# Routing counts by four token columns per product in a fused attention, expert and feed-forward kernel

## The chip, the cores and the metric

The kernel runs on one core of one Trainium2 chip. The metric is the device time of one execution in microseconds (us). An execution is also recorded by the hardware profiler: its span runs from the first to the last instruction. The engines are TensorE (PE in the rows; its weight loads are PEld), VectorE (DVE), ScalarE (ACT), GpSimd (POOL) and SyncE (SP, which issues most transfers).

## The reference

```python
def _moe_ref(x, w_gate, w1, w2):          # x: output of a causal attention with a window of 64
    N, D = x.shape                        # 2304 tokens, 512
    E = w_gate.shape[1]                   # 8 experts
    cap = N // E                          # 288
    flat = (x @ w_gate).flatten()
    order = np.argsort(-flat)
...
    for idx in order:                     # greedy over all (token, expert) pairs
        tok, e = (int(idx) // E, int(idx) % E)
        if assigned[tok] >= 0 or counts[e] >= cap:
            continue
        assigned[tok] = e
        counts[e] += 1
...
    for e in range(E):
        mask = assigned == e
        h = np.maximum(x[mask] @ w1[e], 0.0)
        out[mask] = h @ w2[e]

def _moe2_ref(x, w_in, w_out):            # 512 to 2048 to 512
    h = x @ w_in
    return np.maximum(0.01 * h, h) @ w_out
```

The attention has 4 batches of 8 heads of 576 tokens, 64 wide; each expert is 512 to 1024 to 512.

## The kernel before, in words

**Stages.** The attention takes the first 85 us or so of the span. Then come eight experts, e0 to e7, with 288 tokens each, and the dense feed-forward over blocks of those tokens, m0 to m4, in the order e0 e1 m0 e2 e3 m1 e4 e5 m2 e6 e7 m3 m4. An expert has eight steps, a dense block sixteen. In a step of an expert TensorE does 12 products of 288 columns for `h` and 12 for `ya`; in a step of a block, 12 products of 512 columns for `h` and 12 for `oa` (the weights are `w` or `res`). Each fp32 product is done as three such products, after DVE, ACT or POOL have split the weights into a high and a low part; e0 alone takes its weights unsplit, `w_raw`, in plain fp32.

**Routing.** The greedy assignment is done exactly in eight phases, 0 to 7; phase k fixes the tokens of one more expert, and its gather list must be there before that expert's tokens (`xg`) are fetched by POOL. Tokens lie as 128 partitions by `NT` = 18 columns. A phase below 7 looks for a threshold of each token's key in six rounds, r = 0 to 5. In a round with r of 1 or more:

- DVE compares every key with up to 31 digits: the grid `r_G` (128x558, from `r_E`, the rest of the key, and the last digit in PSUM), and then makes the next `r_E`;
- TensorE counts by expert: one product with `r_nrem` and then 18, one for each token column, whose stationary operand is a 128-column window of the grid and whose moving operand is that column's eight-wide one-hot of the expert, `r_oh`; all add up in one PSUM tile `rp` (128x8);
- DVE makes `r_sat` of it with a scan, and one product with `pow` gives the next digit, again a tile `rp`.

So the chain of a round is: `pow` product, grid and `r_E` on DVE, a burst of 19 products, a scan, the next `pow` product. There is one PSUM buffer for `rp`. A phase ends with a tail on DVE and small products (`r_tot`, `r_OB`, `r_ids`). Round 0 compares the top of the key with 127 values, in pieces along the columns (`cuts`).

**Who sets the order.** No engine looks ahead past a waiting instruction, and the kernel is issued in one hand-made order. `Clocks` keeps a time for each engine as instructions are issued, `cost()` being its price list; `RouteDriver.tick()`, called between the big products, reads these times and puts in the next piece of routing when the model says that its input is ready. `Router.phase` is a generator: `yield 'p'` means that a piece for TensorE comes next, `'v'` one for DVE that waits for TensorE, `'d'` one for DVE that waits for nothing. `tick()` also places pieces of `Convert` (splitting the dense weights) and evacuations. Nearly everything after the attention goes through the helper line L1267, so the rows are told apart by tile names.

Of the kernel before, what the change touches and what calls it, by code (L numbers as in the profile page):

```python
# [8 lines left out]
BF = mybir.dt.bfloat16  # L9
# [4 lines left out]
PSUM = bass.MemoryType.PSUM  # L14
# [3 lines left out]
NT = 18  # L18
# [293 lines left out]
class Router:  # L312
# [3 lines left out]
    def __init__(self, nc, pool, pp, L, cf, ci, cb, ones_b, pow2):  # L316
        self.nc, self.pool, self.pp = nc, pool, pp
        self.cf, self.ci, self.tri, self.iota, self.ones, self.pow2 = cf, ci, cb['tri'], cb['iota'], ones_b, pow2
        self.Lm, self.nps = L, 0
        self.base = pool.tile([128, 2, 8], F32, name="r_base")  # L320
        self.uw = pool.tile([128, 8], F32, name="r_uw")
        self.slotg = pool.tile([128, NT], F32, name="r_slotg")
        self.nrem = pool.tile([128, 8], BF, name="r_nrem")
        self.sel = [pool.tile([128, 128], BF, name=f"r_sel{k}") for k in range(2)]
        for k, x in enumerate(self.sel):
            nc.gpsimd.memset(x, 0.0)
            for p in range(2):
                nc.gpsimd.memset(x[32 * p:32 * p + 1, 1 - k:], 1.0)
        nc.gpsimd.memset(self.sel[0][64:65, 0:1], 1.0)
        self.comb = pool.tile([128, 3], F16, name="r_comb")  # L330
        self.combb = cb['comb']
        self.M = pool.tile([128, 6, NT], I32, name="r_M")
        self.k = pool.tile([128, 2, NT], I32, name="r_k")
        self.spread, self.cont = cb['spread'], cb['cont']
        self.sat = pool.tile([128, 8], BF, name="r_sat")
        self.G = [pool.tile([128, n * NT], BF, name=f"r_G{k}") for k, n in enumerate((128, 38))]
        self.OB = [pool.tile([128, 18 * (n - 1) + 128], F16, name=f"r_OB{n}") for n in (9, 18)]
        for x in self.G + self.OB:
            nc.gpsimd.memset(x, 0.0)
        self.ip = pool.tile([128, 128], F16, name="r_ip")  # L340
# [6 lines left out]
    def start2(self):  # L347
        v, cf = self.nc.vector, self.cf
        v.tensor_copy(self.uw, cf['ew'])
        v.tensor_scalar(out=self.nrem, in0=self.base[:, 0], scalar1=cf['na'], scalar2=cf['nb'], op0=ALU.mult, op1=ALU.add)  # L350
        v.tensor_copy(self.comb, self.combb)
    def ps(self, p, n, apart=False):

        self.nps += 1
        if apart:
            return self.p0.tile([128, 4, 96], F32, tag="xt", name=f"rq{self.nps}", bufs=1).rearrange("p a b -> p (a b)")[:p, :n]
        return self.pp.tile([128, 128], F32, tag="rp", name=f"rp{self.nps}")[:p, :n]
    def t(self, shape, dt, name, ph):
        bufs = {"E": 2, "ids": 8, "eidx": 8}.get(name, 1)
        return self.pool.tile(shape, dt, tag="r_" + name, name=f"r_{name}_{ph}", bufs=bufs)  # L360
# [53 lines left out]
    def phase(self, ph, out):  # L414
# [7 lines left out]
        def b3(ap, n, last):  # L422
            return ap.unsqueeze(2).to_broadcast([128, n, last])
        def bm(ap, n, last):
            return ap.unsqueeze(1).to_broadcast([128, n, last])
        if ph:
            m = t([128, NT], F32, "m", ph)
            v.tensor_reduce(out=m, in_=Lm, axis=AX.X, op=ALU.max)
            eqw = self.eqw0
            TT(out=eqw, in0=Lm, in1=b3(m, NT, 8), op=ALU.is_equal)  # L430
            yield 'd', 0
            TT(out=eqw, in0=eqw, in1=bm(cf['ew'], NT, 8), op=ALU.mult)
            mxw = t([128, NT], F32, "mxw", ph)
            v.tensor_reduce(out=mxw, in_=eqw, axis=AX.X, op=ALU.max)
            OH = t([128, NT, 8], BF, "oh", ph)
            TT(out=OH, in0=eqw, in1=b3(mxw, NT, 8), op=ALU.is_equal)
            yield 'd', 0
        else:
            m, OH, mxw = self.first
        E = dig = None  # L440
        if ph < 7:
            for r in range(6):
                J = 127 if r == 0 else NB[r - 1]
                jw = 128 if J > 32 else 32
                rows = slice(128 - jw, 128 - jw + J)
                GE, win = (self.ge0, self.win0) if ph + r == 0 else self.grid(r % 2, jw)
                pc, c0 = None, 0
                cuts = (0, 18) if ph + r == 0 else (0, 9, 15, 18) if ph == 0 else (0, 9, 18) if r == 0 else (0, 18)
                for lo, hi in zip(cuts, cuts[1:]):
                    w = hi - lo  # L450
                    if r:
                        STT(out=GE[:, lo:hi, :J], in0=b3(E[:, lo:hi], w, J), scalar=dig, in1=bm(cf[f'jt{r - 1}'], w, J), op0=ALU.subtract, op1=ALU.is_ge)
                    elif ph:
                        TT(out=GE[:, lo:hi, :J], in0=b3(m[:, lo:hi], w, J), in1=bm(ci['t1'].bitcast(F32), w, J), op=ALU.is_ge)
                    if hi < NT:
                        yield 'p' if ph == 0 else 'd', 0
                    if hi < NT and ph:
                        continue
                    if hi == NT:
                        if r:  # L460
                            En = t([128, NT], F32, "E", f"{ph}_{r}")
                            if r < 5:
                                STT(out=En, in0=E, scalar=dig, in1=self.M[:, r + 1], op0=ALU.subtract, op1=ALU.add)
                            else:
                                TS(out=En, in0=E, scalar1=dig, scalar2=None, op0=ALU.subtract)
                            E = En
                        elif ph:
                            E = t([128, NT], F32, "E", f"{ph}_0")
                            for _ in self.keys(m, 0, NT, False):
                                pass  # L470
                            self.rest(E)
                        else:
                            E = self.e0
                        yield 'p', 0
                    if pc is None:
                        pc = self.ps(128, 8, ph == 0)
                        nc.tensor.matmul(pc, self.sel[r > 0], self.nrem, start=True, stop=False)
                    for c in range(c0, hi):
                        nc.tensor.matmul(pc, win(c), OH[:, c, :], start=False, stop=(c == NT - 1))
                    c0 = hi  # L480
                yield 'v', 1
                v.tensor_tensor_scan(self.sat[rows], pc[rows], self.ones[rows, :8], 0.0, ALU.max, ALU.min)
                if ph + r == 0:
                    self.rest(E)
                yield 'p', 0
                pa = self.ps(128, 8)
                nc.tensor.matmul(pa, self.pow2[r], self.sat, start=True, stop=True)
                dig = pa[:, 7:8]
                yield 'v', 0
# [692 lines left out]
class Clocks:  # L1182
# [21 lines left out]
    def cost(self, e, name, out, ins):  # L1204
        n = [int(np.prod(x.shape[1:])) for x in [out] + ins]
        psum = any(x.space == PSUM for x in [out] + ins)
        if "dma" in name:
            return 1050 if "indirect" in name else 550 if e == "gpsimd" else 60
        if name == "transpose":
            return n[0] * 0.85  # L1210
        if e == "tensor":
            return max(n[0] * (1.68 if ins[0].dtype == F32 and ins[1].dtype == F32 and ins[1].shape != ins[0].shape else 0.447) + 1, 25)
        n = max(n)
        if e == "scalar":
            return n * 0.833 * (2.9 if out.dtype == F16 else 1) + (55 if psum else 140)
        if e == "gpsimd":
            return n * 2.2 + 98
        big = [x for x in ins if x.shape[-1] > 1]
        fast = not psum and (len(big) < 2 or all(x.dtype == BF for x in big + [out])) and "reduce" not in name
        return n / (1.92 if fast else 0.96) + 66  # L1220
# [4 lines left out]
    def charge(self, e, name, a, kw):  # L1225
# [15 lines left out]
        if e == "tensor":  # L1241
            small = int(np.prod(out.shape[1:])) <= 32
            if self.small and not small:
                end = self.at[e] = end + 90
            self.small = small
        by = e
        if "dma" in name:
# [103 lines left out]
def build(nc, tc, qT, kT, v, vT, wg, cfd, cid, cbd, w12, wio, out):  # L1351
    with ExitStack() as ctx:
# [36 lines left out]
                next(slow, None)  # L1389
        rp = ctx.enter_context(tc.tile_pool(name="rp", bufs=1))  # L1390
        rt = Router(nc, rp, None, L, cf, ci, cb, ones, make_pow2(nc, rp))
        ahead = {5: (0, 6), 11: (6, 12), 14: (12, 15), 17: (15, 18)}
        queue = []
        def done(c):
# [62 lines left out]
```

## Time and profile before

| | |
|---|---|
| time, median of 3 executions | 777.53 us (776.45 to 777.86) |
| time of the profiled execution | 772.07 us |
| its span | 770.4 us |
| mean granted TensorE clock | 0.985 |
| TensorE busy | 735.4 us, 95% of the span |
| TensorE weight loads busy | 622.3 us, 81% |
| VectorE busy | 437.9 us, 57% |
| ScalarE busy | 335.5 us, 44% |
| GpSimd busy | 172.9 us, 22% |

The profiled execution lies 5.46 us under the median of the three timed ones. Busy times are sums over all stages; TensorE's includes time in which products overlap in its pipeline, so pitches (start to start) are read rather than durations.

### The profile page before, as it was taken

How to read it: one execution, taken by the hardware profiler on the slowest of the kernel's cores; microseconds unless marked ns; L12 is line 12 of the kernel's file. 1: busy time of each engine (PE TensorE's matmuls, PEld its weight loads, DVE VectorE, ACT ScalarE, POOL GpSimd, SP SyncE). 2: the span in 40 equal slices, each digit the busy share in tenths (PEclk: the TensorE clock that was granted, in tenths of full speed). 3: DMA queues.
4: the chain of work that ended last, by engine and by line, in shares of the span. 5: the costliest groups of instructions: out<-in, count | busy, mean ns of one | idle time of the engine just before them, and what ended most of it. 6: DMA issues, size and time to landing. Idle time of an engine off the chain costs nothing.

```text
span 770.4 us, 15241 instructions
## 1 busy us (share of the span) xinstructions
PE 735.4 (95%) x5905; PEld 622.3 (81%) x5906; DVE 437.9 (57%) x1110; ACT 335.5 (44%) x736; POOL 172.9 (22%) x263
## 2 busy tenths in 40 slices
PE   6999669999999999999999999999999999999996
PEld 4777436798777789997788899888889998888895
DVE  3798888898899889885832423222233223222332
ACT  4898816566876344432122445222244532121321
POOL 6253130302000024300000598100038830000201
PEclk9999869999999999999999999999999999999999
DMA  9996167624585647362144364622436462324752
GB/s 347 408 412 271 56 213 257 230 75 168 193 268 208 240 159 221 115 220 83 55 164 163 93 211 142 219 91 101 163 110 223 137 219 83 110 76 170 246 180 94
DMA packets 40087, 138.56 MB, mean 180 GB/s; under 512 B 4942, under 2 KB 5966, under 8 KB 40016
## 3 DMA queue, kind: packets, MB, share of 16 engines
q1 hardware_dynamic: 35280, 123.21, 45.7%
q0 software_dynamic: 4304, 14.16, 5.5%
q8 instruction: 46, 0.75, 0.4%
q10 hardware_dynamic: 432, 0.23, 0.1%
q14 instruction: 25, 0.20, 0.1%
HBM read 117.66 MB, written 19.92 MB: 179 GB/s over the span
## 4 chain that ended last, share of the span: by engine, by line
PE 78%; DVE 14%; DMA 4%; issue 2%; ACT 1%; SPq 0%; POOLq 0%; POOL 0%; DVEq 0%; ACTq 0%
PE h L1267 35%; PE oa L1267 24%; PE ya L1267 10%; DVE r_G L1267 3%; PE rp L1267 3%; PE ao L165 2%; DVE w L1267 2%; DMA cv_in<-in_wio_dram 1%; DMA avt<-in_vt_dram 1%; PE apt L150 1%; DVE amx L137 1%; PE xtp L1267 1%; DMA ak<-in_k_dram 1%; PE as L130 1%; PE warm L1267 1%
## 5 line engine op out<-in xcount | busy, mean ns | idle before, releaser
L1267 DVE SCALAR_TENSOR_TENSOR h<-h,tg 128x512 f32<-128x512 f32 (+1 forms) x80 | 51.5, 644 | 149.1 <-ACT tg L1267 148.8
L1267 PE MATMUL h<-Y,w 128*128 128x512 f32 (+1 forms) x600 | 135.3, 371 | 0.0
L1267 PE MATMUL oa<-w,hh 128*128 128x512 f32 x540 | 133.0, 392 | 0.0
L1267 ACT COPY tg<-h 128x512 f32<-128x512 f32 (+1 forms) x80 | 43.6, 545 | 187.6 <-PE h L1267 175.1
L1267 PEld LDWEIGHTS h<-Y,w 128*128 128x128 f32 x600 | 104.2, 188 | 18.6
L1267 PEld LDWEIGHTS oa<-w,hh 128*128 128x128 f32 x540 | 99.7, 188 | 20.0
L1267 POOL TENSOR_TENSOR w<-raw,w 128x512 fp32r<-128x512 f32 x53 | 66.8, 1293 | 207.9 <-DMA raw<-in_w_dram 107.2
L1267 PE MATMUL ya<-hh,w 128*128 128x288 f32 x672 | 99.8, 296 | 0.6 <-DVE hh L1267 0.6
L1267 PE MATMUL h<-xT,w 128*128 128x288 f32 x672 | 100.0, 297 | 0.0
L1267 PEld LDWEIGHTS h<-xT,w 128*128 128x128 f32 x672 | 92.5, 188 | 0.6
L1267 PEld LDWEIGHTS ya<-hh,w 128*128 128x128 f32 x672 | 92.0, 188 | 0.8 <-DVE hh L1267 0.8
L1267 PE MATMUL h<-Y,res 128*128 128x512 f32 (+1 forms) x360 | 82.8, 374 | 0.0
L1267 PE MATMUL oa<-res,hh 128*128 128x512 f32 x324 | 82.2, 398 | 0.0
L1267 POOL DMA_INDIRECT out_dram<-ot,sidx x18 | 19.5, 1082 | 238.5 <-DVE ot L1267 135.6
L1267 DVE TENSOR_TENSOR hh<-h,hh 128x512 fp32r<-128x512 f32 (+1 forms) x80 | 51.0, 637 | 38.5 <-ACT hh L1267 38.3
L1267 PEld LDWEIGHTS h<-Y,res 128*128 128x128 f32 x360 | 62.3, 188 | 12.3
L1267 ACT CAST hh<-h 128x512 fp32r<-128x512 f32 (+1 forms) x80 | 43.6, 545 | 63.9 <-DVE h L1267 63.9
L1267 PEld LDWEIGHTS oa<-res,hh 128*128 128x128 f32 x324 | 59.6, 188 | 13.1 <-ACT hh L1267 0.4
L1267 ACT ACTIVATE hh<-h 128x288 fp32r<-128x288 f32 (+1 forms) x64 | 26.5, 413 | 92.1 <-PE h L1267 90.1
L1267 ACT CAST w<-raw 128x512 fp32r<-128x512 f32 x112 | 64.1, 619 | 0.0
L1267 DVE SCALAR_TENSOR_TENSOR hh<-h,hh 128x288 fp32r<-128x288 f32 x56 | 25.4, 454 | 63.4 <-ACT hh L1267 63.2
L145 ACT ACTIVATE ap<-as,anm 128x128 f32<-128x128 f32 x144 | 41.9, 402 | 17.4 <-DVE anm L138 11.8
(171 smaller groups left out, 935.4 us busy)
## 6 DMA issues: line engine op xcount, KB each, us to landing
w<-wsp SPq DMA_DIRECT2D x80, 512.0 KB, 3.9
raw<-in_w_dram SPq DMA_DIRECT2D x53, 512.0 KB, 4.1
cv_in<-in_wio_dram SPq DMA_DIRECT2D x32, 512.0 KB, 5.2
wsp<-w SPq DMA_DIRECT2D x20, 512.0 KB, 3.7
avo<-in_v_dram SPq DMA_DIRECT2D x6, 876.0 KB, 9.9
aq<-in_q_dram SPq DMA_DIRECT2D x12, 384.0 KB, 9.7
avt<-in_vt_dram SPq DMA_DIRECT2D x6, 768.0 KB, 9.9
xd<-ax SPq DMA_DIRECT2D x18, 256.0 KB, 7.7
```

Of the source, the lines that this page charges most:

```text
L130: nc.tensor.matmul(S[64 * t:64 * t + 64, a, u, :].rearrange("p (b c) -> p b c", b=2), q[h], k[h], start=False, stop=True, skip_group_check ...
L137: nc.vector.tensor_reduce(out=mx, in_=S[:, a:a + n], axis=AX.X, op=ALU.max)
L145: nc.scalar.activation(p[:, u, :], S[:, a, u, :], AF.Exp, bias=nm[a][:, u:u + 1], scale=0.125)
L150: nc.tensor.transpose(pt[:, u, :], p[:, u, :], ident)
L165: nc.tensor.matmul(o[64 * t:64 * t + 64, h // 4, h % 4, :], ptb[:, u, 64 * t:64 * t + 64], (ve, vo)[t][m][:, s, h, :], start=True, stop=Tr ...
L1267: return f(*a, **kw)
```

## The change

Three things in `Router`, and the price list of the model that orders everything:

- In phases 2 to 6, rounds 1 to 5 (25 rounds), the burst of 19 products becomes two bursts of five. The first, A, multiplies a window of the grid with the one-hots of four token columns at once (32 columns; the last product 16); of its 128x32 result only a shifted diagonal counts. ACT copies the result to `r_cq` as f16, and the second burst, B, is the `r_nrem` product and four products with shifted identities (`r_shift`), which add up the diagonal in the 128x8 tile. Other products run between A and B. `r_shift` is filled once, by GpSimd and DVE, during the attention.
- Three small DVE operations on the keys move from behind round 0's grid to between the operations ahead of it, in phases 1 to 6; round 0's grid is made in three pieces instead of two.
- `Clocks.cost` gets other prices for DVE scans and strided reads, for operations with a scalar in PSUM and for small f16 outputs on ACT; a big product behind a small one is charged 30 ns, not 90.

```diff
@@ Router.__init__ / start2
+        self.shift = pool.tile([128, 224], F16, name="r_shift")
+        nc.gpsimd.memset(self.shift, 0.0)
...
+        v.tensor_copy(self.shift[:, 96:], self.ident)
@@ Router.phase
             eqw = self.eqw0
+            ks = self.keys(m, 0, NT, False) if ph < 7 else iter(())
             TT(out=eqw, in0=Lm, in1=b3(m, NT, 8), op=ALU.is_equal)
+            next(ks, 0)
             yield 'd', 0
             TT(out=eqw, in0=eqw, in1=bm(cf['ew'], NT, 8), op=ALU.mult)
+            next(ks, 0)
...
-                cuts = (0, 18) if ph + r == 0 else (0, 9, 15, 18) if ph == 0 else (0, 9, 18) if r == 0 else (0, 18)
+                cuts = (0, 18) if ph + r == 0 else (0, 9, 15, 18) if ph == 0 else (0, 6, 12, 18) if r == 0 else (0, 18)
...
-                            for _ in self.keys(m, 0, NT, False):
-                                pass
                             self.rest(E)
...
+                    if ph > 1 and r:
+                        pb = self.ps(128, 32)
+                        for k in range(0, NT, 4):
+                            n = min(4, NT - k)
+                            nc.tensor.matmul(pb[:, :8 * n], self.G[r % 2][:, 96 + 32 * k:224 + 32 * k], OH[:, k:k + n, :], start=(k == 0), stop=(k >= NT - 6), skip_group_check=True)
+                        yield 'v', 1
+                        cq = t([128, 32], F16, "cq", f"{ph}_{r}")
+                        nc.scalar.copy(cq, pb)
+                        yield 'p', 0
+                        pc, c0 = self.ps(128, 8), hi
+                        nc.tensor.matmul(pc, self.sel[1], self.nrem, start=True, stop=False)
+                        for k in range(4):
+                            nc.tensor.matmul(pc, self.shift[:, 32 * k:32 * k + 128], cq[:, 8 * k:8 * k + 8], start=False, stop=(k == 3))
@@ Clocks.cost / charge
-            return n * 0.833 * (2.9 if out.dtype == F16 else 1) + (55 if psum else 140)
+            return n * 0.833 * (2.9 if out.dtype == F16 and n > 100 else 1) + (55 if psum else 140)
...
+        if "scan" in name or max((x.ap[-1][0] for x in ins if x.shape[-1] > 1), default=1) > 4:
+            return n * 2.1 + 66 if n > 100 else n + 66
+        if any(x.space == PSUM and x.shape[-1] == 1 for x in ins):
+            return n / 0.96 + 140
...
-                end = self.at[e] = end + 90
+                end = self.at[e] = end + 30
```

TensorE in block m1, a round of phase 6, before (`rp_5537` is the count of round 2; 17 more pairs like the last one follow, the number behind a row is how many follow one another):

```order
L1267 LDWEIGHTS pow_1_93
L1267 MATMUL rp_5524<-r_sat,pow_1_93 128x8
L1267 MATMUL oa_2_5485<-res_72,hh_5462 128x512
L1267 MATMUL oa_3_5486<-res_72,hh_5462 128x512
L1267 MATMUL h_5533<-Y_0_1_1850,res_73 128x512
L1267 MATMUL h_5533<-Y_0_1_1858,res_73 128x512
L1267 MATMUL h_5533<-Y_0_1_1850,res_73 128x512
L1267 LDWEIGHTS r_sel_113
L1267 MATMUL rp_5537<-r_nrem,r_sel_113 128x8
L1267 LDWEIGHTS r_G_125
L1267 MATMUL rp_5537<-r_oh_5369,r_G_125 128x8
```

The same round of phase 6 in m1 after the change (`rp_5638` is burst A, `rp_5653` burst B; left out are three more pairs of A, four more rows of `oa` and two more pairs of B):

```order
L1289 LDWEIGHTS pow_1_93
L1289 MATMUL rp_5622<-r_sat,pow_1_93 128x8
...
L1289 LDWEIGHTS r_G_127
L1289 MATMUL rp_5638<-r_oh_5521,r_G_127 128x32
L1289 MATMUL rp_5638<-r_oh_5521,r_G_127 128x16
L1289 MATMUL oa_3_5167<-w_55_5453,hh_5548 128x512 x2
...
L1289 LDWEIGHTS r_sel_113
L1289 MATMUL rp_5653<-r_nrem,r_sel_113 128x8
L1289 LDWEIGHTS r_shift
L1289 MATMUL rp_5653<-r_cq_2_5646,r_shift 128x8
L1289 MATMUL h_5661<-Y_0_1_1853,w_57_5528 128x512
```

Ten small products stand in two places instead of 19 in one; six `oa` products stand between A and B here, three in some other rounds.

TensorE in e0, a round of phase 1, before (one of these rows of `h` is one fp32 product, which the trace shows as two; 17 more pairs of `rp_2313` follow the last row):

```order
L1267 LDWEIGHTS pow_2_96
L1267 MATMUL rp_2306<-r_sat,pow_2_96 128x8
L1267 MATMUL h_2303<-xT_0_2181,w_raw_2086 128x288 x2
L1267 LDWEIGHTS r_sel_113
L1267 MATMUL rp_2313<-r_nrem,r_sel_113 128x8
L1267 LDWEIGHTS r_G_126
L1267 MATMUL rp_2313<-r_oh_2178,r_G_126 128x8
```

The same round in e0 after the change:

```order
L1289 LDWEIGHTS pow_2_96
L1289 MATMUL rp_2311<-r_sat,pow_2_96 128x8
L1289 MATMUL h_2282<-xT_0_2188,w_raw_2089 128x288 x2
L1289 MATMUL ya_0_2320<-hh_2276,w_raw_2087 128x288
L1289 LDWEIGHTS r_sel_113
L1289 MATMUL rp_2325<-r_nrem,r_sel_113 128x8
L1289 LDWEIGHTS r_G_128
L1289 MATMUL rp_2325<-r_oh_2184,r_G_128 128x8
```

Three fp32 products stand between `pow` and the burst instead of two; the burst itself is the old one in phase 1.

## Rows read from the trace of the kernel before

**Rows 1.** Stretches: length, then busy us of PE, PEld, DVE, ACT, POOL; clock.

```profile
145.00:760.00 615.00, 612.72 (x3950) 529.91 (x3950) 321.15 (x761) 237.95 (x477) 119.47 (x167) 1.00 0.47 158
200.00:250.00 50.00, 49.85 (x285) 39.23 (x284) 46.70 (x108) 34.73 (x60) 0.00 (x0) 1.00 0.68 233
```

**Rows 2.** Operations on tile rp: ns min/median/max, first and last start.

```profile
L1267 PE MATMUL rp<-r_oh,r_G x648: 166/166/168, 110.8 to 362.3; 128*128 128x8 bf16 x162
```

**Rows 3.** Timeline of PE, two half steps of a block without routing: start, us.

```profile
405.93 2.88 PE L1267 MATMUL h<-Y,w 128*128 128x512 f32 x12
408.65 2.96 PE L1267 MATMUL oa<-res,hh 128*128 128x512 f32 x12
```

**Rows 4.** Timeline of PE in m0: a pow product, then a burst.

```profile
208.51 0.61 PE L1267 MATMUL oa<-w,hh 128*128 128x512 f32 x2
208.96 0.18 PE L1267 MATMUL rp<-r_sat,pow 128*128 128x8 bf16 x1
...
211.38 1.52 PE L1267 MATMUL h<-Y,w 128*128 128x512 f32 x6
...
212.78 0.59 PE L1267 MATMUL rp<-r_oh,r_G 128*128 128x8 bf16 x18
...
214.72 0.63 PE L1267 MATMUL oa<-res,hh 128*128 128x512 f32 x2
```

**Rows 5.** Timeline of PE in an expert, steps without routing.

```profile
446.69 1.74 PE L1267 MATMUL ya<-hh,w 128*128 128x288 f32 x12
448.27 1.75 PE L1267 MATMUL h<-xT,w 128*128 128x288 f32 x12
```

**Rows 6.** Timeline of PE in e3: a burst among `ya`, a pow product among `h`.

```profile
302.62 1.21 PE L1267 MATMUL ya<-hh,w 128*128 128x288 f32 x8
...
303.72 0.59 PE L1267 MATMUL rp<-r_oh,r_G 128*128 128x8 bf16 x18
...
304.79 0.96 PE L1267 MATMUL h<-xT,w 128*128 128x288 f32 x6
305.59 0.18 PE L1267 MATMUL rp<-r_sat,pow 128*128 128x8 bf16 x1
...
306.51 0.66 PE L1267 MATMUL xtp<-ident,xg 96*128 96x96 f32 x6
```

**Rows 7.** Timeline of all engines in e0, a round of phase 1.

```profile
116.59 1.22 PE L1267 MATMUL h<-xT,w_raw 128*128 128x288 f32 x4
116.80 0.81 DVE L1267 SCALAR_TENSOR_TENSOR r_G<-r_E,rp,cft 128x558 bf16<-128x558 f32 x1 [0.45 <-PE rp L1267]
117.52 0.23 DVE L1267 SCALAR_TENSOR_TENSOR r_E<-r_E,rp,r_M 128x18 f32<-128x18 f32 x1
117.81 0.10 PEld L1267 LDWEIGHTS <-r_sel 128*128 128x128 bf16 x1 [0.46 <-DVE r_E L1267]
```

**Rows 8.** Timeline of PE in e0: four such products with no burst behind.

```profile
123.52 1.22 PE L1267 MATMUL h<-xT,w_raw 128*128 128x288 f32 x4
124.57 1.13 PE L1267 MATMUL ya<-hh,w_raw 128*128 128x288 f32 x4
```

**Rows 9.** Groups of instructions: count, busy us, mean ns, idle before.

```profile
L1267 PEld LDWEIGHTS h<-Y,w 128*128 128x128 f32 x600 | 104.2, 188 | 18.6
L1267 ACT CAST Y<-ya 128x32 fp32r<-128x32 f32 x4 | 0.7, 187 | 2.2 <-PE ya L1267 2.2
L1267 ACT COPY tg<-h 128x512 f32<-128x512 f32 x64 | 37.6, 587 | 164.4 <-PE h L1267 151.9 <-PE rp L1267 12.4
L1267 ACT ACTIVATE cv_in<-cv_in 128x512 f16<-128x512 f32 x10 | 13.7, 1370 | 0.2
```

**Rows 10.** The gather of expert 1's tokens: its last issue, landing times, the use.

```profile
135.63 0.92 POOL L1267 DMA_INDIRECT xg<-xd,r_ids  x1 [0.30 <-issue]
DMA to landing us min/median/max: 3.1/5.1/6.8
147.85 0.83 PE L1267 MATMUL xtp<-ident,xg 96*128 96x96 f32 x8
```

More of the change, by code (lines that the diff above doesn't have):

```diff
@@ L335, in __init__ @@
         self.sat = pool.tile([128, 8], BF, name="r_sat")
-        self.G = [pool.tile([128, n * NT], BF, name=f"r_G{k}") for k, n in enumerate((128, 38))]
+        self.G = [pool.tile([128, n * NT], BF, name=f"r_G{k}") for k, n in enumerate((128, 41))]
         self.OB = [pool.tile([128, 18 * (n - 1) + 128], F16, name=f"r_OB{n}") for n in (9, 18)]
@@ L429, in phase @@
             eqw = self.eqw0
+            ks = self.keys(m, 0, NT, False) if ph < 7 else iter(())
             TT(out=eqw, in0=Lm, in1=b3(m, NT, 8), op=ALU.is_equal)
+            next(ks, 0)
             yield 'd', 0
             TT(out=eqw, in0=eqw, in1=bm(cf['ew'], NT, 8), op=ALU.mult)
+            next(ks, 0)
             mxw = t([128, NT], F32, "mxw", ph)
             v.tensor_reduce(out=mxw, in_=eqw, axis=AX.X, op=ALU.max)
+            next(ks, 0)
             OH = t([128, NT, 8], BF, "oh", ph)
@@ L1391, in build @@
         rt = Router(nc, rp, None, L, cf, ci, cb, ones, make_pow2(nc, rp))
+        rt.ident = ident
         ahead = {5: (0, 6), 11: (6, 12), 14: (12, 15), 17: (15, 18)}
```

## The prediction

> **What bounds the kernel now.** I read the busy time by stretches first. From 145 to 760 us of the span TensorE is busy for 612.72 of 615 us at full granted clock, and from 200 to 250 us, block m0, for 49.85 of 50 us although DVE is busy there for 46.70 and ACT for 34.73 us [rows 1]. The reader is to see that TensorE is the bound of everything behind the routing of expert 0, that it waits for almost nothing (2.3 us in all), and that a DVE near its limit does not hold it up. So an edit in phases 2 to 6 is worth what it takes off TensorE's own stream, plus or minus what it makes TensorE wait. The operations on the routing tile came next: a counting product takes 166 ns from start to end, 648 of them up to 362.3 us [rows 2]. That is a latency; what a product costs the stream has to be read from starts. Last I read TensorE's timeline in four places (steps of a block and of an expert, with and without routing), and all engines through one round of phase 1.
>
> **The price of small products.** A half step of twelve 512-column products without routing goes from 405.93 to 408.65: 2.72 us [rows 3]. The half step of `oa` that holds one `pow` product goes from 208.51 to 211.38: 2.87, so one lone small product costs 0.15 us. The half step of `h` that holds a burst of 19 goes from 211.38 to 214.72: 3.34, so the burst costs 0.62 [rows 4]. With a fixed part a for leaving and taking up the big products again, and b for each small one, a + b = 0.15 and a + 19b = 0.62: b = 0.026 and a = 0.124. In an expert, twelve 288-column products take 446.69 to 448.27, 1.58 us [rows 5]; with a burst 302.62 to 304.79, 2.17, and with a `pow` 304.79 to 306.51, 1.72 [rows 6]. So 0.59 and 0.14: b = 0.025, a = 0.115. The b agrees with the burst's own row, 18 products in 0.59 us of which the last takes 0.166: 0.42/17 = 0.025 [rows 2, 4].
>
> **What the change takes off.** A round of phases 2 to 6 had one burst of 19 and gets two bursts of five: ten products instead of 19, but the fixed part twice. In a block 2 x (0.124 + 5 x 0.026) = 0.51 instead of 0.62, a gain of 0.11; in an expert 2 x (0.115 + 5 x 0.025) = 0.48 instead of 0.59, also 0.11. With 25 rounds **-2.75 us**. Nine products saved per round would be 0.23 us; about half goes to the second entry. That A's products have 32 columns instead of eight is not in the trace of before; I give them the same b, because a 512-column product has a pitch of 2.72/12 = 0.227 us, and 32/512 of that is 0.014, less than b. The bounds of this term: a free second entry gives 25 x 0.23 = 5.8; a second entry that costs a whole exposed weight load of a big product, 0.188 us [rows 9], gives 25 x (0.23 - 0.19) = 1.0.
>
> A load of a small product's weights lasts 0.10 us [rows 7], and yet the products of a burst start every 0.025 us and those of a plain half step every 0.227 with loads of 0.188 [rows 3, 4, 9]: the loads lie beside products in flight. The Trainium skill ("TensorE: Matmul & The Clock Gate", section "What overlaps and what doesn't") says that a weight load overlaps products in flight only when its row group differs, and these are all full height. By that rule nine loads fewer in a round would be 9 x 0.10 x 25 = 22.5 us in place of the 2.75, and the forecast 754.5; the pitches just named speak against it, and it gets a chance of 0.01, inside the first rival.
>
> **What the corrected clocks give.** In phase 1 the burst waits. `pow` ends, DVE makes the grid (0.81 us) and the rest `r_E` (0.23), and the burst's first weight load starts at 117.81, 0.06 behind `r_E`'s end, with `r_E` named as what was waited for [rows 7]. The two fp32 products put in as cover (four rows) run from 116.59 to 117.81, 1.22 us; where no burst follows, the same four rows take 123.52 to 124.57, 1.05 [rows 8]. So 0.17 us of each such round is a wait that the busy time hides. The order after the change has three fp32 products there, 1.57 us of cover by the same pitch, and the wait is gone. Five rounds: **-0.85 us**, with 0 as the bound if another wait, the scan's, takes its place. Phase 1's own chain gets longer by this, since a round now has more work of e0 in it: the gather list of expert 1 comes some seven fp32 products (3.6 us) later in e0's work, less the waits saved and with the phase's other steps drawn together, by my count about 2 us later in time. The last gather was issued by 135.63 + 0.92 and lands 5.1 us later in the median, at 141.65; its tokens are first used at 147.85 [rows 10]. Phase 2's rounds, which lay ahead of that use, now lie mostly behind it, so that the use comes about 2 us earlier, near 145.8. A slack of 6.2 us shrinks to some 2, and to 0.5 with the slowest landing, 6.8. I cost it at nothing, with the bound at 1 us.
>
> **What lies beside other work.** The copy to `r_cq` is 25 small ACT operations. ACT's own 128x32 copy out of PSUM took 0.187 us; a 128x512 to f16 took 1.37 where an fp32 copy took 0.59, a factor of 2.3 [rows 9], so one copy is 0.19 to 0.44, 4.7 to 11 us in all on an engine that TensorE rarely waits for. I take 0.19 to 0.25, since the small row is mostly fixed cost. The copy matters only through B, which waits for it: 0.17 for A's last product, about 0.06 for each of two hand-overs [rows 2, 7], and the copy: 0.48 to 0.73. Between A and B the new order has three 512-column products in seven rounds (0.68 us, to which A's own pitch behind its last start adds a fixed part of 0.12), six 288-column ones in seven (0.79 + 0.12), and more in eleven. So an ACT that is free when A ends hides the copy everywhere. In m0 it is busy seven tenths of the time [rows 1], so some copies queue; the driver's model knows ACT's queue and puts in more cover, and I leave +0.2 for what it misjudges. The key operations on DVE change place, not number; round 0's grid gets one more piece, five or six times a few tens of nanoseconds on an engine whose 46.70 of 50 us did not hold TensorE up; without that cover it is +0.3. The cast that fills `r_shift` is one DVE operation in the attention: +0.1. DVE has the same operations otherwise. The routing of phases 2 to 7 moves later, by half an expert to a whole one, but each list is still ready some steps before its expert: nothing.
>
> **Sum.** -2.75 - 0.85 + 0.2 + 0.1 + the pieces' nothing = -3.3 us against the profiled execution's 772.07: 768.8. That execution was 5.46 us below the median of the three timed, 777.53; taken over to the median the forecast is **774.2 us**, 0.42% less.
>
> **Rivals.**
> *More than that.* TensorE still has 2.3 us of idle time behind 145 us [rows 1], and I left it. If the new clocks remove most of it, or the second entry costs less than a, the gain is 5 to 6.5 us: 771 to 772.5. For it: the waits have the cause that the clocks' new prices are about, DVE operations that the model held too short. Against: an entry is an entry, and each `pow` row pays it.
> *The second entry eats the gain.* Each return to the big products would expose a whole weight load, 0.188 us [rows 9], and the shifted identities another wait; the products saved leave 25 x 0.04 = 1.0, and a late scan keeps the waits of phase 1: 776.5, within 0.2% of before. For it: two entries instead of one in every round, so the change could trade one cost for another of the same size. Against: a lone `pow` costs 0.15 or 0.14 in all, its own b included [rows 4, 6], less than 0.188.
> *Slower: B waits for ACT's copy.* ACT takes its instructions in order. In the 14 rounds with short cover, a copy that lands behind one evacuation or conversion of 512 columns comes up to 0.59 us later [rows 9]. Need then 0.48 + 0.59 = 1.07, cover 0.80 or 0.91: 0.16 to 0.27 us; with the dear copy (0.44) 0.41 to 0.52. The gain of 3.3 is used up at 0.24 us per round over 14 rounds, and it is slower by more than 0.2% from 0.35 us per round on. With the dear copy and ACT busy each time, 14 x 0.46 = 6.4: 780.6. For it: ACT's 34.73 of 50 us in m0, and this wait did not exist before. Against: half of these rounds lie in experts, where ACT is mostly idle, and the order was made with ACT's queue in the model.
>
> **How the numbers follow.** Some 0.2% (1.55 us) is what a measurement of this kernel can tell from no change. The forecast, 772.5 to 775.9: 0.57. More: 0.14. The entry eats the gain, 775.98 to 778.5: 0.19; this holds a partial wait for the copy too. Slower: 0.10, with the seam at expert 1's gather as a small part. So faster 0.71, same 0.19, slower 0.10. The range takes in the gain from a free entry at one end and the second rival at the other: 770.6 to 778.3, leaving out the slower case and the ends, under 0.2.
>
> **What would show it.** Right: a stream with 25 fewer bursts of 19; in a block, a half step with A alone and one with B alone each about 0.25 us above 2.72; the four-row cover of phase 1 grown to six rows at 1.05/4 us each with no pitch left over; no idle time of TensorE before a weight load of `r_shift`, or under 0.2 us in the sum. Wrong: idle time of TensorE with ACT's `r_cq` as its end; small products of 32 columns at a pitch well over 0.026; a half step with A or B at 0.3 or more; a wait of the `xtp` products of expert 1 for their gather; or rounds of phases 2 to 6 whose `pow` now waits for the scan, since fewer big products stand behind B than stood behind the burst.

## The result, and the profile after

The changed kernel takes 766.7 us (median of 4, 765.1 to 768.1) where the kernel before takes 777.67 (776.45 to 777.86): a ratio of 0.9862, interval 0.9833 to 0.989. That is faster, as forecast, but by 10.97 us where 3.3 were forecast, and below the range. The profiled execution took 768.13 us. Page of the changed kernel, its span, part 1 and the chain:

```profile
span 766.4 us, 14817 instructions
PE 731.0 (95%) x5680; PEld 616.6 (80%) x5681; DVE 438.7 (57%) x1120; ACT 337.9 (44%) x761; POOL 169.8 (22%) x261
PE 85%; DVE 9%; DMA 2%; ACT 1%; issue 1%; POOLq 0%; POOL 0%; SPq 0%; DVEq 0%; ACTq 0%
```

The profile on record of before has a span of 770.4 us, only 4.0 more: two executions, one of each, show less than half of what the medians show. That is the first thing that has to be explained. Operations on the routing tile after the change (columns as in [rows 2]):

```profile
L1289 PE MATMUL rp<-r_oh,r_G x323: 166/166/190, 112.7 to 396.7; 128*128 128x8 bf16 x99, 128*128 128x32 bf16 x50, 128*128 128x16 bf16 x13
L1289 PE MATMUL rp<-r_cq,r_shift x100: 166/166/167, 150.1 to 397.9; 128*128 128x8 f16 x100
L1289 ACT CAST r_cq<-rp x25: 158/186/202, 148.3 to 397.3; 128x32 f16<-128x32 f32 x25
```

The first row mixes three shapes. By shape (columns as in [rows 9]):

```profile
L1289 PE MATMUL rp<-r_oh,r_G 128*128 128x32 bf16 x100 | 6.6, 179 | 0.0
L1289 PE MATMUL rp<-r_oh,r_G 128*128 128x8 bf16 x198 | 6.5, 166 | 0.0
```

A product with 32 columns lasts 179 ns in the mean, 13 ns more than one with eight, and the copy 0.186 us in the median, the lower end of the forecast's 0.19 to 0.44. TensorE's timeline in e1, a round of phase 2, with burst A and burst B:

```profile
160.32 0.56 PE L1289 MATMUL h<-xT,w 128*128 128x288 f32 x3
160.72 0.28 PE L1289 MATMUL rp<-r_oh,r_G 128*128 128x32 bf16 x5
160.86 1.04 PE L1289 MATMUL h<-xT,w 128*128 128x288 f32 x6
161.74 0.18 PE L1289 MATMUL rp<-r_nrem,r_sel 128*128 128x8 bf16 x1
161.78 0.24 PE L1289 MATMUL rp<-r_cq,r_shift 128*128 128x8 f16 x4
161.88 0.65 PE L1289 MATMUL h<-xT,w 128*128 128x288 f32 x3
162.37 0.43 PE L1289 MATMUL ya<-hh,w 128*128 128x288 f32 x2
```

The half step of `h` goes from 160.32 to 162.37, 2.05 us against 1.58 without routing [rows 5]: both entries together 0.47, forecast 0.48, where the burst of 19 cost 0.59 [rows 6]. A's five products start 0.028 us apart ((0.28 - 0.17)/4). In blocks, the trace has four half steps with A and no other small product, 3.03 us in the median, and two with B and no other, 3.01; the plain ones take 2.75 in the median, so that is 0.29 and 0.26 (forecast 0.25 each). The 2.72 of [rows 3] is the shortest plain half step; over it A alone stands at 0.31, just beyond the forecast's own sign of being wrong. A round of phase 1 in e0, where [rows 7] showed the wait:

```profile
118.53 1.22 PE L1289 MATMUL h<-xT,w_raw 128*128 128x288 f32 x4
119.58 0.65 PE L1289 MATMUL ya<-hh,w_raw 128*128 128x288 f32 x2
120.06 0.17 PE L1289 MATMUL rp<-r_nrem,r_sel 128*128 128x8 bf16 x1
```

Six rows from 118.53 to 120.06, 1.53 us at 0.255 each: no wait is left in them. All that TensorE waits for from 112 to 760 us (in total, times, the longest), and the one of the three waits that lies in e2:

```profile
PE rp L1289 <- ACT r_cq L1289: 1.7, 3, 0.8
```

```profile
290.18 0.17 PE L1289 MATMUL rp<-r_nrem,r_sel 128*128 128x8 bf16 x1 [0.59 <-ACT r_cq L1289]
```

**An account by stages.** A stage runs from its first `h` product to that of the next, as TensorE's timeline has them. From its length I take the price of the small products that stand in it: entries times 0.124 or 0.115 us and products times 0.0256, the prediction's a and b, the counts from the same timeline. The rest is big products, which are the same in all kernels, and waits, shown or hidden in busy time. "Second" is experiment 1, "third" is experiment 11, on another chip. The last row ends with TensorE's last product, some 7 us before the span does.

| stage: length (small products) rest, us | before, on record | before, second | after, on record | after, third |
|---|---|---|---|---|
| start of e0 | 112.34 | 113.58 | 114.20 | 112.65 |
| e0, e1 | 70.48 (9.93) 60.55 | 70.45 (9.93) 60.52 | 65.54 (8.63) 56.91 | 65.53 (8.63) 56.90 |
| m0 | 97.33 (10.20) 87.13 | 97.73 (10.20) 87.53 | 93.13 (5.67) 87.46 | 92.51 (5.67) 86.84 |
| e2, e3 | 60.91 (6.05) 54.86 | 63.63 (6.05) 57.58 | 60.79 (5.36) 55.43 | 60.79 (5.36) 55.43 |
| m1 | 93.37 (6.38) 86.99 | 93.34 (6.38) 86.96 | 96.53 (10.17) 86.36 | 96.53 (10.17) 86.36 |
| e4 to the last product | 328.70 | 328.71 | 328.94 | 328.93 |

Stages without routing give the scale: e4 and e5 take 54.5 us, m2 86.5 to 86.7. From the second profile of before to the third of after: small products 32.56 to 29.83, **-2.7**; rest of e0 and e1 **-3.6**; rest of e2 and e3 **-2.2**; m0 and m1 -0.7 and -0.6 (of which TensorE's recorded idle time is 0.8 and 0.2); start of e0 -0.9; the end +0.2. The sum is -10.5, and the spans are 774.7 and 764.2. The start of e0 varies by some 2 us between executions of one kernel (112.34 and 113.58 before, 114.20, 112.41 and 112.65 after), so I count it as no part of the change.

### The profile page after: what moved, and what is told of

The parts are those of the page before. It is cut to its first block, busy times and chain, and to the rows that moved or that the text cites. A ratio compares the mean times of both kernels' runs of the same rounds, so it can differ in the third digit from the quotient of the medians.

```text
span 766.4 us, 14817 instructions
## 1 busy us (share of the span) xinstructions
PE 731.0 (95%) x5680; PEld 616.6 (80%) x5681; DVE 438.7 (57%) x1120; ACT 337.9 (44%) x761; POOL 169.8 (22%) x261
## 4 chain that ended last, share of the span: by engine, by line
PE 85%; DVE 9%; DMA 2%; ACT 1%; issue 1%; POOLq 0%; POOL 0%; SPq 0%; DVEq 0%; ACTq 0%
PE h L1289 38%; PE oa L1289 24%; PE ya L1289 14%; PE rp L1289 2%; PE ao L165 2%; PE apt L150 1%; DVE r_G L1289 1%; DVE amx L137 1%; PE xtp L1289 1%; PE as L130 1%; DMA avt<-in_vt_dram 1%; DMA cv_in<-in_wio_dram 1%; PE warm L1289 1%; DVE cv_r L1289 1%; PE rq L1289 1%
## 5 line engine op out<-in xcount | busy, mean ns | idle before, releaser
L1289 POOL TENSOR_TENSOR w<-raw,w 128x512 fp32r<-128x512 f32 x50 | 63.0, 1295 | 194.3 <-ACT w L1289 193.9
L1289 POOL DMA_INDIRECT out_dram<-ot,sidx x18 | 22.5, 1250 | 219.2 <-DVE ot L1289 216.1
L145 ACT ACTIVATE ap<-as,anm 128x128 f32<-128x128 f32 x144 | 41.8, 401 | 17.6 <-DVE anm L138 11.5
```

What stands on the lines that cost most here:

```text
L145: nc.scalar.activation(p[:, u, :], S[:, a, u, :], AF.Exp, bias=nm[a][:, u:u + 1], scale=0.125)
L1289: return f(*a, **kw)
```

## The experiments

Experiments 1 to 4, 5 to 8, 9 to 12 and 13 to 15 ran on a chip each; before took 777.4, 773.7, 778.0 and 777.9 us on them, so each kernel is compared with before on its own chip. Each expectation sets two theories of its own, A and B, against each other. At first they were, in the main, that the parts of the forecast add up and one profile of before was odd (A), or that the order as a whole decides (B).

**1. Before, again.** No edit.

> The unchanged kernel before, for a second profile. Theory A (one execution was odd): the profiled execution of 772.07 us was not a typical one of this kernel, and the others, at 777.5, lose some 5.5 us in one place, most likely where the tokens of expert 0 or 1 arrive, since the start of e0 already differs by 1.86 us between the two profiles on record. Then the time is 777.5 and a new profile at 777 shows 5 to 6 us more in one stretch between 100 and 185 us. Theory B (spread): the 5.5 us lie all over the span, as a lower granted clock would make it; then every stage of the new profile is 0.5 to 1% longer.

Measured: ratio 1.000 (0.9977 to 1.0024), 777.54 us, profiled 776.35. Compared with the first profile, e0 starts 1.24 us later and e2 with e3 is 2.72 us longer; the other stages agree within 0.4. So theory A, in two places rather than one, and the larger one later than expected: the execution on record lay under all 35 of before on this chip (774.63 to 780.62). It need not be an odd execution of one chip: on the chip of experiments 5 to 8 before takes 772.12 to 775.81, and the record doesn't say on which chip the first profile was taken. What is new in e2, on ACT and TensorE:

```profile
288.57 1.14 ACT L1267 CAST w<-raw 128x512 fp32r<-128x512 f32 x2
293.22 0.41 ACT L1267 ACTIVATE hh<-h 128x288 fp32r<-128x288 f32 x1 [3.51 <-remote]
```

```profile
289.26 1.75 PE L1267 MATMUL h<-xT,w 128*128 128x288 f32 x12
```

The same place in the profile of before on record:

```profile
287.67 1.75 PE L1267 MATMUL h<-xT,w 128*128 128x288 f32 x12
289.52 0.41 ACT L1267 ACTIVATE hh<-h 128x288 fp32r<-128x288 f32 x1 [1.40 <-PE h L1267]
```

There `h` ends at 289.42 and ACT starts 0.1 us later. In the second profile the `h` that ACT waits for is through by 291.01 on TensorE's record, and ACT starts 2.2 us later, with no recorded instruction as its releaser (the trace calls that remote). The Trainium skill ("Perfetto Trace Analysis", section "Tensor Engine Instruction (MATMUL, LD_WEIGHTS)") says that a product's end is estimated by the profiler, and that its semaphore is pushed after PSUM has acknowledged the write, so a late result can't be read from TensorE's own rows. The trace agrees: the late result shows in the waiting engine's start, and in the record of the semaphore's update, at 293.14, 0.08 us ahead of that start.

**2 to 4. One part alone, one part away.** Experiment 2 is before with the new `Clocks.cost` and the penalty of 30. Experiment 3 is before with the four-column products alone. Experiment 4 is the changed kernel without them:

```diff
# 2: before, and all lines of the change in class Clocks, as
+            return n * 0.833 * (2.9 if out.dtype == F16 and n > 100 else 1) + (55 if psum else 140)
...
+                end = self.at[e] = end + 30
# 3: after, and back again class Clocks, the place of keys() and
-                cuts = (0, 18) if ph + r == 0 else (0, 9, 15, 18) if ph == 0 else (0, 6, 12, 18) if r == 0 else (0, 18)
+                cuts = (0, 18) if ph + r == 0 else (0, 9, 15, 18) if ph == 0 else (0, 9, 18) if r == 0 else (0, 18)
# 4: after, and
-                    if ph > 1 and r:
+                    if ph > 99 and r:
```

> The kernel before with only the new price list of the driver's model. Theory A (the prediction's terms): the price list removes waits of the phase 1 rounds and no more, -0.85 to -2 us, 775.5 to 776.7. Theory B (the price list carries most of the gain, since it moves phase 2's rounds out of e0 and draws the waits out of e0 and e1, where the stages of the two profiles differ by 4.9 us): 767.5 to 771.

> The kernel before with only the four-column products in phases 2 to 6; price list, key operations and pieces of round 0 as before. Theory A: -2.75 us from 25 rounds at 0.11 us, plus or minus a wait, 774 to 776. Theory B (the order is what counts, the product next to nothing): 776.5 to 778.5, or slower if waits for the r_cq copy come in under the old prices.

> The changed kernel without the four-column products (bursts of 19 in all phases); price list, key operations and pieces of round 0 as changed. Theory A: 2.75 us above the changed kernel's 766.7, that is 769 to 770, if the parts add up. Theory B (products next to nothing): 766.5 to 767.5. If the parts hang together in another way, by a gather that comes late or not, the time jumps by 3 us or more: 772 or above.

Measured: price list alone 775.77, ratio 0.9973 (0.9958 to 0.9988); products alone 774.41, 0.9966 (0.9949 to 0.9984), 3.0 us, as forecast for the products; all but the products 777.35, 0.9999 (0.9982 to 1.0015). By the time alone, experiments 2 and 3 come out as theory A, and 4 as the third case of its expectation. The parts do not add up: 1.6 and 3.0 us alone, 11.0 the whole change, and everything but the products nothing. (The third part, the key operations and the pieces of round 0, was not run alone.) The stages say why. The rest of e0 and e1 is 57.06 us with the price list alone, 61.00 with the products alone, so the price list removes 3.5 us there. But the rest of e2 and e3 goes up to 61.50 with the price list and 60.87 in experiment 4, where 54.5 is clean. (The profiled execution of experiment 2, 779.31 us, was the slowest of its twelve, so the median pays less than this.) TensorE in experiment 2:

```profile
285.11 0.59 PE L1271 MATMUL rp<-r_oh,r_G 128*128 128x8 bf16 x18
285.56 0.77 PE L1271 MATMUL ya<-hh,w 128*128 128x288 f32 x4
290.77 0.17 PE L1271 MATMUL rp<-r_sat,pow 128*128 128x8 bf16 x1 [4.44 <-DVE r_sat L1271]
```

A `pow` product waits 4.44 us for a scan whose count was through by 285.70.

**5. After, again.** No edit.

> The changed kernel once more, for more executions and a second profile. Theory A (an account of the stages holds for all executions): 766 to 768.5, with the product's gain and the waits of e0 and e1 removed in every execution. Theory B (the four executions on record were lucky): 770 or more.

Measured: 765.01 us, ratio 0.9884 (0.9869 to 0.9899). The executions on record were not lucky ones. The gain on this chip is 8.7 us, 2.3 less than on record; before is faster here.

**6 to 8. Away from the late count.** Experiment 6 (on the kernel of experiment 4) places no routing in the first four steps of e2. Experiments 7 (on that of 4) and 8 (on the changed one) queue m0's four stores for e3:

```diff
# 6
+            R.block = first[2] <= i < first[2] + 4        # tick() places no piece of routing meanwhile
# 7, 8
-                    sc = nc.gpsimd.indirect_dma_start(out=self.out, ...
+                    if n: scatter()
+                    else: self.lates.append(scatter)      # the same two instructions
...
+            while i == first[2] + 8 and self.lates: self.lates.pop(0)()
```

> The changed kernel without the four-column products (777.4), and with no piece of routing placed in the first four steps of e2, where its profile and that of the price list alone show TensorE idle for 2.9 and 4.4 us before a pow product and then 6.8 us at half the granted clock. Theory A (that one wait, met by a round with a short chain behind a burst, costs the 5 to 8 us that the new clocks lose again): 769.5 to 772, with no such idle time. Theory B (the delay is in the stage whatever stands there, and moves to the next instruction that waits): 776 to 778.

> The changed kernel without the four-column products, and with the four indirect stores of m0's output put behind expert 3's gather, in e3 instead of at the start of e2. Theory A (TensorE's results are seen late while GpSimd issues those stores and the gather behind them): no idle time of 2 us or more before a pow product in e2, 769.5 to 772. Theory B (the stores have nothing to do with it): the wait stays, 776 to 778.

> The changed kernel with the four indirect stores of m0's output in e3 instead of at the start of e2. Theory A: the changed kernel pays only about 1 us there (0.59 us before an r_cq product), so -0.5 to -1.5 us, 765 to 766.5. Theory B: nothing, 766.5 to 768, or slower by the stores' later place.

Measured: 771.37 (0.9967, 0.995 to 0.9983), 769.94 (0.9941, 0.9924 to 0.9959) and 765.93 (0.9891, 0.9874 to 0.9909; the changed kernel beside it 0.9884). GpSimd was free at the end of m0, so in experiments 7 and 8 the stores still went out at 279 to 288 us; what the edit moved is expert 3's gather, which no longer waits behind them and went out in m0, from 257.3 and 269.1 us on. In experiments 6 and 7 the rest of e2 and e3 is 54.27 and 54.21, clean; in 8 nothing is gained. As a proof this is weak: on this chip none of the four profiles shows a late count, and the kernel of experiment 4 did not run there.

**9 to 12. The same on one chip.** The kernels of experiments 4, 7, the changed one, and that of 3, with no new edit.

> The changed kernel without the four-column products, again, now on one chip with the two that it has to be compared with. Theory A (at the start of e2 a pow product waits for a scan that sees TensorE's counts late, in many executions and on some chips): a wide spread, and on average 5 to 8 us above the same kernel with late stores; the same as before or up to 3 us below it. Theory B (the product's gain alone lies between this and the changed kernel): 2.7 us above the changed kernel, no wait before a pow product in e2.

> The same with the four indirect stores of m0 in e3. Theory A: 5 to 8 us below the kernel without late stores, some 4 to 5 above the changed kernel (2.7 us of products and the 1.7 us that a burst waits in m0). Theory B: the same as the kernel without late stores, within 1 us.

> The changed kernel as a mark on the same chip: 1.1 to 1.4% below before by either theory, 764 to 768 as the chip goes.

> The kernel before with the four-column products alone, on the same chip as the others. Theory A (parts add up where no wait of the second kind is met): 2.5 to 4 us below before, some 6 to 7 above the changed kernel (3.6 us of waits in e0 and e1 that the price list removes, the rest waits in m0 to m1). Theory B: within 2 us of before.

Measured, with before at 778.04: 777.11 (0.9992, 0.9972 to 1.0011); 771.57 (0.9924, 0.9898 to 0.995); 766.58 (0.9864, 0.9837 to 0.989); 775.98 (0.9969, 0.9952 to 0.9986). So theory A in experiments 9 to 11: the order of one gather on GpSimd is worth 5.5 us to the kernel without the products. Experiment 12 fits neither theory: it is 2.1 us below before, where A said 2.5 to 4, and 9.4 above the changed kernel, where A said 6 to 7. Its e2 and e3 have 3.2 us of idle time, so late results cost the products too when the prices are the old ones. Experiment 9 in e2, in this order: TensorE, DVE, GpSimd, then stretches with the columns of [rows 1], whose seventh value is the granted clock:

```profile
286.71 0.59 PE L1289 MATMUL rp<-r_oh,r_G 128*128 128x8 bf16 x18
287.16 1.30 PE L1289 MATMUL ya<-hh,w 128*128 128x288 f32 x8
288.30 0.56 PE L1289 MATMUL h<-xT,w 128*128 128x288 f32 x3
292.59 0.17 PE L1289 MATMUL rp<-r_sat,pow 128*128 128x8 bf16 x1 [3.72 <-DVE r_sat L1289]
```

```profile
292.36 0.18 DVE L1289 TENSOR_TENSOR_SCAN r_sat<-rp,ones 31x8 bf16<-31x8 f32 x1 [3.63 <-remote]
```

```profile
282.83 1.00 POOL L1289 DMA_INDIRECT out_dram<-ot,sidx  x1 [95.24 <-DVE ot L1289]
...
286.68 1.37 POOL L1289 DMA_INDIRECT out_dram<-ot,sidx  x1 [0.21 <-issue]
288.35 1.20 POOL L1289 DMA_INDIRECT xg<-xd,r_ids  x1 [0.30 <-issue]
...
291.10 0.92 POOL L1289 DMA_INDIRECT xg<-xd,r_ids  x1 [0.30 <-issue]
```

```profile
284.00:289.00 5.00, 4.13 (x44) 3.62 (x43) 2.78 (x6) 2.36 (x5) 4.13 (x6) 1.00 0.49 189
289.00:292.50 3.50, 0.00 (x0) 0.00 (x0) 0.14 (x1) 0.00 (x0) 2.59 (x4) 0.79 0.85 248
292.50:297.00 4.50, 4.41 (x19) 4.41 (x19) 4.37 (x12) 1.44 (x3) 1.76 (x5) 0.50 0.69 194
```

The count is through by 287.30 on TensorE's record; the scan starts at 292.36, 5.06 us later, when GpSimd has just issued the last of seven indirect transfers in a row. DVE is held at the scan, TensorE at the `pow` behind it for 3.72 us; the granted clock falls to its lower level, 1.2 GHz, while TensorE stands idle, and products take about twice their time until some 298 us. That is 61.53 in place of 54.5 for the rest of e2 and e3. In experiment 10, with the gather out of the row, the same round:

```profile
283.91 0.59 PE L1296 MATMUL rp<-r_oh,r_G 128*128 128x8 bf16 x18
...
285.50 0.55 PE L1296 MATMUL h<-xT,w 128*128 128x288 f32 x3
287.66 0.17 PE L1296 MATMUL rp<-r_sat,pow 128*128 128x8 bf16 x1 [1.61 <-DVE r_sat L1296]
```

The scan is late still, and the `pow` waits 1.6 us for it, but the clock keeps its level, and the rest of e2 and e3 is 56.06.

**13 to 15. Stores or gather, and does before pay?** Experiment 13 is the kernel of 4 as a mark. Experiment 14 leaves m0's four stores out, so that 512 rows of the output are missing. Experiment 15 is before with experiment 7's edit alone:

```diff
# 14: as 7, but
-            while i == first[2] + 8 and self.lates: self.lates.pop(0)()
# 15: before, and as 7
+            while i == first[2] + 8 and self.lates: self.lates.pop(0)()
```

> The changed kernel without the four-column products, as the mark on this chip for the next run. Either theory: within 0.3% of before, with one scan in e2 that sees TensorE's counts 3 to 5 us late if the chip is of the kind where that happens.

> The same without the four indirect stores of m0's output (those 512 rows of the output are left out), so that expert 3's gather, which waits behind them, goes out in m0. Theory A (counts are seen late while GpSimd has stores and a gather in a row under way): no late scan in e2, 5 to 7 us below the kernel with stores. Theory B (late counts come with the step into e2 whatever GpSimd does): no difference, a late scan of 3 to 5 us. Between the two: if the gather had been enough by itself, the late scan moves into m0.

> The kernel before with expert 3's gather put ahead of m0's stores in GpSimd's order, nothing else. Theory A (before pays for late counts too, some 2 to 3 us in e2 and e3 as its second profile shows, and its first profile was one without): -1.5 to -3.5 us. Theory B (only the order with the new clocks meets them): within 0.8 us of before.

Measured, with before at 777.94: 775.72 (0.9984, 0.9954 to 1.0015); 769.89 (0.9898, 0.9867 to 0.9928); 775.35 (0.9972, 0.9949 to 0.9995). Without stores no scan is late and the rest of e2 and e3 is 54.22, 60.48 in experiment 13: 5.8 us by the times. The same round in experiment 14, where the count is through by 284.68:

```profile
284.09 0.59 PE L1294 MATMUL rp<-r_oh,r_G 128*128 128x8 bf16 x18
285.38 0.18 DVE L1294 TENSOR_TENSOR_SCAN r_sat<-rp,ones 31x8 bf16<-31x8 f32 x1
286.09 0.18 PE L1294 MATMUL rp<-r_sat,pow 128*128 128x8 bf16 x1
```

Before gains by the order of one gather too, 0.28% or 2.2 us with an interval that goes from 0.4 to 4.0, as it should if it pays for late results. The gather alone, in m0, costs TensorE no wait in experiments 14 and 15. With stores alone (experiment 10) the scan starts 2.9 us behind its count's end; with stores and gather in a row 4.2 to 5.1 in the same kernel and in that with the price list alone.

The trace also records when each semaphore was updated. In experiment 9 the next update of TensorE's semaphore behind the count's end at 287.30 comes at 292.33, 0.02 us ahead of the scan. From 110 to 760 us, five of the 17 profiles have no update of it that comes more than 0.6 us behind the last recorded end before it: before on record, and experiments 5 to 8. The other twelve have five to twelve such updates each, also near 445 and 590 us, where the stores of m1 and m2 and a gather go out and no routing waits. In experiment 14 they stand at 446 and at 582 to 587 us alone, and none is left where m0's stores were. DVE and ACT have none in any profile.

## Why the prediction was wrong

**The products: right.** "With 25 rounds -2.75 us": the kernel with the products alone gained 3.0 and 2.1 us. The account's -2.73 only counts entries and pieces at the forecast's own prices; that these hold shows in what they leave: 54.50 us for e2 and e3 in experiments 5 and 8, as in stages without routing, and 54.2 with bursts of 19 in experiments 7 and 14. The second entry costs a, as taken, not 0 and not a whole weight load of 0.188 us. The rule of the Trainium skill ("TensorE: Matmul & The Clock Gate", section "What overlaps and what doesn't") that a weight load overlaps products in flight only when its row group differs, from which the prediction got 22.5 us, does not hold for these: the runs show 2.1 to 3.0.

**The clocks: the mis-sized term.** "Five rounds: -0.85 us" counted the waits ahead of five bursts of phase 1. The price list removed all recorded waits of e0 and e1 and hidden ones too: 3.6 us by the account, 3.5 by experiment 2 against 1. Of these, 1.6 us stood as recorded idle time in the trace of before in those two stages, 1.1 of it in two rows:

```profile
162.89 0.18 PE L1267 MATMUL rp<-r_tot,cbt 128*128 128x16 bf16 x1 [0.48 <-DVE r_tot L1267]
181.40 1.58 PE L1267 MATMUL ya<-hh,w 128*128 128x288 f32 x10 [0.60 <-DVE hh L1267]
```

The prediction saw 2.3 us of idle time in [rows 1] and left it to a rival with a chance of 0.14. The other 2.0 us were hidden in busy time, where the prediction had found 0.85. The cause that this rival names, DVE operations priced too short, fits experiment 2; that run changes the prices of DVE, of ACT and of a small product together, so which of them did it isn't separated.

**The base: the step that failed.** "That execution was 5.46 us below the median [...]; taken over to the median" assumed that what an execution pays beyond its profile is paid by both kernels alike. It isn't. The execution on record is of the kind without late results, 0.4 us over clean in e2 and e3; the second profile pays 3.1 us there for results that are seen late, and the order of one gather takes 2.2 of before's time away (experiment 15, 0.4 to 4.0). The changed kernel pays 0.9 there in two of its three profiles (the 0.59 us wait shown above) and nothing in the third. That is another 2.2 us. The chips say the same: 8.7 us of gain on the one without late results (experiment 5), 11.5 on that of experiments 9 to 12. What is left between the forecast's 3.3 and the account's 10.5 is mostly the 1.3 us in m0 and m1, 1.0 of it recorded idle time that the new order doesn't have, and the 0.9 at the start of e0, which is luck of these two executions.

**The sum as a sum.** "-2.75 - 0.85 + 0.2 + 0.1" treats the parts as independent. They aren't: with the new prices and bursts of 19, a short chain of a round falls into the row of stores and gather, and the 6 to 7 us lost there eat the 3.6 won in e0 and e1. With the four-column products and the new prices together the late stretch holds no such stop: in the three profiles of the changed kernel one count or none is late there, by 1.24 us. Why the lateness itself is shorter in that order than with bursts of 19 isn't settled; it wasn't separated from where the rounds stand in the row.

**The rivals.** "More than that" was the nearest (771 to 772.5), and still 4 us short. "The second entry eats the gain" is refuted by experiments 3 and 12. "B waits for ACT's copy" happens three times for 1.7 us in all (0.2 was left for it) and in other executions for 0.2 and 0.8; it was never near 0.24 us per round. The seam at expert 1's gather shows no wait, as costed. There is a wait that no rival named: in m0 without the products a burst waits up to 2 us for `r_E`, while DVE is on conversion pieces. In the profiles of experiments 6 and 9 the granted clock falls to 1.2 GHz for 3.4 us behind it, and m0's rest is 90.2 and 89.7 us. Row of experiment 7, where it doesn't:

```profile
225.46 0.18 PE L1296 MATMUL rp<-r_nrem,r_sel 128*128 128x8 bf16 x1 [1.66 <-DVE r_E L1296]
```

Between experiments 10 and 11 (771.57 and 766.58) the account has 2.7 us of small products, and 2.0 from the rests of m0, e2 with e3, and m1.

## What to carry to other kernels

Take the profiled execution's own waits apart from the median's before costing a change: if it lies far from all timed executions, a second profile shows where the difference sits, and the changed kernel need not pay for it too. When a kernel's order comes from a model of the engines, a part tried alone may show nothing: here two parts worth 1.6 and 3.0 us alone belong to a whole worth 11.0. One of them moves a stop into a bad place (experiments 2, 4, 9), and with both it is gone, by what means isn't shown. Subtract small products by entry and piece from a stage's length, and what is left shows waits that busy time hides.

## What the runs showed of the hardware

TensorE's results were seen 1.2 to 5.1 us after their recorded end while GpSimd issued four indirect stores and three gathers in a row, on ACT and on DVE, in experiments 1, 2, 3, 4, 9, 12 and 13 and in two of the three profiles of the changed kernel. In experiments 5 and 6, which ran on one chip, and in the execution of before on record the same row of seven stands in the trace and nothing is late, so the row alone is not enough; what differs there isn't known. In experiment 9 the lateness ended 0.3 us behind the last issue. It is shown that it goes when the stores go (experiment 14, with late updates at the later stores of the same execution), and shrinks when the gather goes ahead (10). What holds the results back isn't shown. TensorE's semaphore updates are late and those of DVE and ACT are not, but TensorE's ends are estimates, so whether the products' writes or only the semaphores are late can't be read from these traces. In experiment 9 the granted clock fell from 2.4 to 1.2 GHz in an idle stretch of TensorE of 3.7 us: of the 7.0 us that e2 and e3 are longer than clean, 4.4 are recorded idle time, and the rest, 2.6, goes with the clock. In experiment 10 an idle stretch of 1.6 us there was not followed by a lower clock; in m0 one of 1.5 us was (experiment 9) and one of 1.9 us was not (experiment 14).
